# A two-block decode attention kernel: filler matmuls ahead of each exp, and the V products in one run

## The chip, the cores and the metric

The kernel runs on one core of one Trainium2 chip. The metric is device time in microseconds (us) of one execution; three runs of the kernel before gave 2033.15, 2031.56 and 2034.47 us, median 2033.15 us. The core's engines are named as in the profile: PE is TensorE (matmuls), PEld its weight loads, DVE VectorE, ACT ScalarE, POOL GpSimd, and SP the engine whose queue issues the transfers. "Clock" means the TensorE clock that the throttle granted, as a share of full speed.

## The reference

Two attention blocks, A and B, of the same shape; each is one decode step (one query position) over a cache:

```python
B, Sq, D = 2, 1, 640;  H, Sk, Dh = 32, 8192, 192        # bf16
q = (x @ wq).reshape(B, Sq, H, Dh).transpose(0, 2, 1, 3)
scores = jnp.einsum("bhqd,bhkd->bhqk", q, k_cache) * (Dh ** -0.5)
p = softmax(scores, axis=-1)
o = jnp.einsum("bhqk,bhkd->bhqd", p, v_cache)
out = o.transpose(0, 2, 1, 3).reshape(B, Sq, H * Dh) @ wo   # A and B concatenated
```

K and V are 2 x 32 x 8192 x 192 bf16 for each block, and every element is used once. The four caches are 805.3 MB of the 836.77 MB that the profile counts as read.

## The kernel before

The 2 blocks x 2 batches x 32 heads are handled two heads at a time: 64 **pairs**, i = 0 to 63. One pair's K is one transfer of 6144 KB into a buffer of 128 partitions (64 for each head, 128 positions in each), and so is its V. Three such buffers (`ring`, line 86) are filled in turn in the order K0, V0, K1, V1, ..., V61, K62, K63, V62, V63 (lines 155 to 169). All these transfers are issued by SP (line 134), strictly in that order, and each waits until the buffer's last contents have been used: by this rotation **K of pair i+2 waits for the last V product of pair i**, and **V of pair i+1 waits for the last multiplication of K of pair i**. Two loads of `wq` lead the stream, and eleven pieces of `wo` end it, in the buffers of K63, V62 and V63.

The order on each engine is written out by hand in the loop at line 382; each engine has a stream of its own, and waits are semaphores.

For pair i: K is taken in four quarters. `add_mul` (DVE, line 233) multiplies a quarter by the broadcast query into one of two `prod` buffers. `add_sum` (PE, line 238) adds the products over the head dimension, in 12 matmuls with the identity, each 128x512 moving columns, into one of two PSUM tiles `scps`. `add_red` (DVE, line 245) reduces the 16 columns that are left to scores. The DVE order is multiply 0, multiply 1, reduce 0, multiply 2, reduce 1, multiply 3, reduce 2, reduce 3; multiply 2 needs the buffer that sum 0 reads. `add_max` takes the maximum (DVE lines 250 and 251, POOL line 254), `add_exp` the exponentials (ACT, lines 259 to 266). `add_l` (PE, line 284) sums the denominators; it is the first PE instruction that waits for exp.

`add_pv` is the V product: 64 matmuls (line 278), each loading 34 columns of probabilities as weights and streaming 384 columns of V. Before the change it is cut in three: 52 matmuls follow `add_l` of the same pair, 6 follow sum 0 of the next pair and 6 follow sum 1 of the next pair. Only the last of the 64 signals `("pv", i)`, for which K of pair i+2 waits on SP. `add_od` and `add_on` (ACT line 294, DVE lines 298 to 302) normalise the output, and `add_place` (PE, line 312) puts it into the transposed layout for `wo`. `add_contract` (PE, line 327) multiplies by `wo` at the end.

Of the kernel before, what the change touches and what calls it, by code (L numbers as in the profile page):

```python
# [8 lines left out]
BF16 = mybir.dt.bfloat16  # L9
F32 = mybir.dt.float32  # L10
# [41 lines left out]
def build_kernel(nc, blocks, out):  # L52
# [8 lines left out]
    T = 128  # L61
# [19 lines left out]
    with ExitStack() as es:  # L81
        sb = lambda name, shape, dt: es.enter_context(nc.sbuf_tensor(name, shape, dt))
        ps = lambda name, shape, dt: es.enter_context(nc.psum_tensor(name, shape, dt))
# [17 lines left out]
        ident = sb("ident", [128, 128], BF16)  # L101
        selb = sb("selb", [34, 2, 128], BF16)
        place = sb("place", [2, 264], BF16)
        ones = sb("ones", [128, 1], F32)
        oallS = [sb(f"oallS{k}", [128, WR, 2], BF16) for k in range(NBLK)]
        out_sb = [sb(f"out_sb{k}", [34, NH2], BF16) for k in range(NBLK)]
        actd = sb("actd", [128, 2], F32)
# [3 lines left out]
        qps = ps("qps", [128, 512], F32)  # L111
        oall = ps("oall", [128, 512], F32)
        outps = ps("outps", [128, 512], F32)

        reg = {}
        S_sp = _Stream("sp", sem("s_sp"), reg)
        S_pe = _Stream("pe", sem("s_pe"), reg)
        S_act = _Stream("act", sem("s_act"), reg)
        S_dve = _Stream("dve", sem("s_dve"), reg)
        S_pool = _Stream("pool", sem("s_pool"), reg)  # L120
# [69 lines left out]
        def pr3(qd):  # L190
            return prod[qd % 2][:].rearrange("p (t d) -> p t d", d=Dh)

        def key(name, i, *rest):
            return (name, i) + rest if i >= 0 else None

        def before(i, qd, n):
            k = 4 * i + qd - n
            return (k // 4, k % 4) if k >= 0 else None
# [29 lines left out]
        def add_mul(i, qd):  # L228
            q = qt[i % 3][:].unsqueeze(1).broadcast_to([128, TQ, Dh])
            prev = before(i, qd, 2)  # L230
            w = [("k", i), ("qt", i)]
            w += [("s",) + prev] if prev else [("pr", 0, NQC - 1), ("pr", 1, NQC - 1)]
            S_dve.add(lambda eng: eng.tensor_tensor(pr3(qd), quarter(i, qd), q, ALU.mult), waits=w, sig=("m", i, qd))  # L233

        def add_sum(i, qd):
            def fn(eng):
                for j in range(NJ):
                    ins = eng.matmul(scps[qd % 2][:], ident[:], pr3(qd)[:, :, j * DG:(j + 1) * DG],  # L238
                                     start=(j == 0), stop=(j == NJ - 1))
                return ins  # L240
            prev = before(i, qd, 2)
            S_pe.add(fn, waits=[("m", i, qd), ("init",), ("r",) + prev if prev else None], sig=("s", i, qd))

        def add_red(i, qd):
            S_dve.add(lambda eng: eng.tensor_reduce(sc[i % 2][:, qd * TQ:(qd + 1) * TQ], scps[qd % 2][:], AXL.X, ALU.add),  # L245
                      waits=[("s", i, qd), key("exp", i - 2)], sig=("r", i, qd))

        def add_max(i):
            def fn(eng):
                eng.tensor_reduce(mp[i % 2][0:64, 0:1], sc[i % 2][0:64, :], AXL.X, ALU.max)  # L250
                return eng.tensor_reduce(mp[i % 2][64:128, 1:2], sc[i % 2][64:128, :], AXL.X, ALU.max)  # L251
            S_dve.add(fn, waits=[("r", i, 0), ("r", i, 1), ("r", i, 2), ("r", i, 3), key("ar", i - 2), ("init",)],
                      sig=("mx", i))
            S_pool.add(lambda eng: eng.partition_all_reduce(mg[i % 2][:], mp[i % 2][:], 128, bass.bass_isa.ReduceOp.max),  # L254
                       waits=[("mx", i), key("nb", i - 2)], sig=("ar", i))

        def add_exp(i):
            def fn_nb(eng):
                eng.activation(nb[i % 2][0:64, :], mg[i % 2][0:64, 0:1], ACTF.Identity, scale=-scale)  # L259
                return eng.activation(nb[i % 2][64:128, :], mg[i % 2][64:128, 1:2], ACTF.Identity, scale=-scale)  # L260
            S_act.add(fn_nb, waits=[("ar", i), key("exp", i - 2)], sig=("nb", i))

            def fn(eng):
                for h in range(2):
                    p0 = 64 * h
                    ins = eng.activation(pb[i % 2][p0:p0 + 64, :, h::32],  # L266
                                         sc[i % 2][p0:p0 + 64, :].rearrange("p (j a) -> p j a", a=2),
                                         ACTF.Exp, bias=nb[i % 2][p0:p0 + 64, :], scale=scale,
                                         accum_out=rs[i % 2][p0:p0 + 64, h:h + 1])
                return ins  # L270
            S_act.add(fn, waits=[("nb", i), ("r", i, 3), key("pv", i - 2), key("l", i - 2), ("init",)], sig=("exp", i))

        def pv_part(i, j0, j1):
            vv = ring[slot_of["v", i]][:].rearrange("p (j f) -> p j f", f=2 * Dh)

            def fn(eng):
                for j in range(j0, j1):
                    ins = eng.matmul(ops[i % 2][0:34, 0:2 * Dh], pb[i % 2][:, j, :], vv[:, j, :],  # L278
                                     start=(j == 0), stop=(j == T // 2 - 1))
                return ins  # L280
            return fn

        def add_l(i):
            S_pe.add(lambda eng: eng.matmul(ops[i % 2][0:2, 448:449], rs[i % 2][:], ones[:], start=True, stop=True),  # L284
                     waits=[("exp", i), key("on", i - 2), ("qe", 1, NQC - 1), ("init",)], sig=("l", i))

        def add_pv(i, j0, j1):
            w = [("exp", i), ("v", i)]
            if i == LAST and j0:
                w.append(("v2", i))  # L290
            S_pe.add(pv_part(i, j0, j1), waits=w, sig=("pv", i) if j1 == T // 2 else None)

        def add_od(i):
            S_act.add(lambda eng: eng.activation(oodd[i % 2][:], ops[i % 2][32:34, Dh:2 * Dh], ACTF.Identity),  # L294
                      waits=[("pv", i), key("on", i - 2)], sig=("od", i))

        def add_on(i):
            S_dve.add(lambda eng: eng.reciprocal(rc[i % 2][:], ops[i % 2][0:2, 448:449]),  # L298
                      waits=[("l", i), ("pv", i), key("on", i - 2)], sig=("rc", i))
            S_dve.add(lambda eng: eng.tensor_tensor(oodd[i % 2][:], ops[i % 2][0:2, 0:Dh], oodd[i % 2][:], ALU.add),  # L300
                      waits=[("od", i)], sig=("ad", i))
            S_dve.add(lambda eng: eng.tensor_scalar(on[i % 2][:], oodd[i % 2][:], rc[i % 2][:], None, ALU.mult),  # L302
                      waits=[("rc", i), ("ad", i), key("pl", i - 2)], sig=("on", i))
# [42 lines left out]
        for blk in range(NBLK):  # L346
# [5 lines left out]
        S_pool.add(lambda eng: eng.affine_select(out=place[:], in_=place[:], compare_op=ALU.is_equal, fill=0.0, base=-128,  # L352
                                                 pattern=[[1, 264]], channel_multiplier=-4), waits=[("pl0",)])
        S_pool.add(lambda eng: eng.memset(ones[:], 1.0))
        for t in rs + pb:
            S_pool.add((lambda t: lambda eng: eng.memset(t[:], 0.0))(t))
        for t in mp:
# [7 lines left out]
        def fn_x(eng):  # L365
            for c in range(DC):
# [4 lines left out]
                  waits=[("xp",)], sig=("xT",))  # L371
# [5 lines left out]
                    add_q(i)  # L377
                    add_qt(i)

        J = T // 2  # L380
        J1, J2 = J - 12, J - 6
        for i in range(NP):
            mid = 0 < i < LAST
            add_mul(i, 0)
            add_mul(i, 1)
            add_sum(i, 0)
            if mid:
                add_pv(i - 1, J1, J2)
            add_red(i, 0)
            add_mul(i, 2)  # L390
            add_sum(i, 1)
            if mid:
                add_pv(i - 1, J2, J)
                add_od(i - 1)
            add_red(i, 1)
            add_mul(i, 3)
            add_sum(i, 2)
            add_red(i, 2)
            if mid:
                add_on(i - 1)  # L400
            if i + 2 < NP:
                add_q(i + 2)
                add_qt(i + 2)
            add_sum(i, 3)
            if mid:
                add_place(i - 1)
            add_red(i, 3)
            add_max(i)
            add_exp(i)
            if i < NP - 2:  # L410
                add_l(i)
                add_pv(i, 0, J1)
        for i in (NP - 2, NP - 1):
            add_l(i)
            if i == LAST:
                add_pv(i, 0, J // 2)
                add_pv(i, J // 2, J)
            else:
                add_pv(i, 0, J)
            add_od(i)  # L420
            add_on(i)
            if i == NP - 2:
                add_place(i)
# [77 lines left out]
```

## Time and profile before

| what | value |
|---|---|
| median of three runs | 2033.15 us (2031.56 to 2034.47) |
| the profiled execution, its own time | 2037.92 us |
| its span, first to last instruction | 2036.1 us |
| read from memory | 836.77 MB, 411 GB/s over the span |
| PE, DVE, ACT busy | 1616.5 us (79%), 1081.5 us (53%), 187.1 us (9%) |
| packets' time of the loading queue, share of 16 engines | 97.1% |
| mean granted TensorE clock | 0.916 |

Busy times of PE come from records whose ends are modelled, so 79% is no measure of how near PE is to its limit. The share of the DMA engines is the time that packets took; a packet that takes longer than others makes this share larger and not the transfer faster, so GB/s is to be read beside it.

### The profile page before, as it was taken

Reading aid. Unit: us, or ns where it says so; the run is one execution under the profiler, and the core shown is the slowest. Engines: PE = TensorE matmul, PEld = TensorE weight load, DVE = VectorE, ACT = ScalarE, POOL = GpSimd, SP = SyncE. Lnnn points to the kernel's source line nnn. Section 1 sums busy time; section 2 is a strip of 40 time slices with the busy share of each in tenths; the row PEclk is TensorE's granted clock in tenths of the full one; section 3 lists DMA queues with packets and bytes.
Section 4 is the critical chain, followed back from the end, with each engine's and each line's share of the span. In section 5 each row is a group of like instructions: output and inputs, shape, how many; then the busy total and the mean of one; then the engine's idle time right before and its main releaser. Section 6 shows DMA issues by size and latency. Waiting matters only on the chain.

```text
span 2036.1 us, 17767 instructions
## 1 busy us (share of the span) xinstructions
PE 1616.5 (79%) x7933; PEld 748.8 (37%) x7933; DVE 1081.5 (53%) x833; ACT 187.1 (9%) x610; POOL 32.2 (2%) x82
## 2 busy tenths in 40 slices
PE   5878887878878887887878878887877777877877
PEld 1333333333333433333333333333333333333334
DVE  0645655645655655655655645645645645645660
ACT  2101001001011001001001001001001001001000
POOL 1000000000000000000000000000000000000000
PEclk9998988888998988989888988988999999898989
DMA  9999999999999999999999999999999999999998
GB/s 414 430 409 416 404 430 394 402 427 406 402 431 406 424 410 416 404 427 421 403 418 417 408 428 398 416 405 405 404 426 419 403 421 402 390 426 393 426 401 381
DMA packets 20836, 837.91 MB, mean 412 GB/s; under 512 B 2316, under 2 KB 2584, under 8 KB 2968
## 3 DMA queue, kind: packets, MB, share of 16 engines
q1 hardware_dynamic: 20744, 836.78, 97.1%
q8 instruction: 62, 1.02, 0.2%
q14 instruction: 14, 0.11, 0.0%
q10 hardware_dynamic: 16, 0.01, 0.0%
HBM read 836.77 MB, written 0.01 MB: 411 GB/s over the span
## 4 chain that ended last, share of the span: by engine, by line
issue 62%; DMA 20%; PE 12%; DVE 5%; POOL 1%; SPq 0%; ACT 0%; POOLq 0%; DVEq 0%
DMA ring<-in_B_k_cache_dram 17%; PE scps L238 7%; DVE prod L233 4%; PE ops L278 4%; DMA prod<-in_B_wq_dram 2%; DMA ring<-in_B_wo_dram 1%; PE ops L205 1%; POOL mg L254 1%; DVE sc L245 0%; SPq L134 0%; ACT pb L266 0%; POOLq L43 0%; DVE mp L251 0%; PE ops L284 0%; ACT out_sb L335 0%
## 5 line engine op out<-in xcount | busy, mean ns | idle before, releaser
L233 DVE TENSOR_TENSOR prod<-ring,qt 128x6144 bf16<-128x6144 bf16 x256 | 852.7, 3351 | 757.9 <-DMA ring<-in_B_k_cache_dram 354.3
L238 PE MATMUL scps<-prod,ident 128*128 128x512 bf16 x3072 | 762.5, 402 | 172.6 <-DVE prod L233 170.4
L278 PE MATMUL ops<-ring,pb 128*34 128x384 bf16 x4096 | 788.1, 354 | 0.0
L278 PEld LDWEIGHTS ops<-ring,pb 128*34 128x34 bf16 x4096 | 416.0, 105 | 359.9 <-issue 151.4
L238 PEld LDWEIGHTS scps<-prod,ident 128*128 128x128 bf16 x3072 | 292.1, 102 | 592.5 <-DVE prod L233 213.1
L245 DVE TENSOR_REDUCE sc<-scps 128x32 f32<-128x512 f32 x256 | 175.7, 686 | 147.0 <-PE scps L238 146.8
L284 PE MATMUL ops<-ones,rs 128*2 128x1 f32 x128 | 12.2, 164 | 211.8 <-ACT pb L266 211.8
L294 ACT ACTIVATE oodd<-ops 2x192 f32<-2x192 f32 x64 | 20.6, 321 | 1323.0 <-PE ops L278 1323.0
L284 PEld LDWEIGHTS ops<-ones,rs 128*2 128x2 f32 x128 | 5.5, 82 | 219.3 <-ACT pb L266 218.8
L266 ACT ACTIVATE pb<-sc,nb 64x128 bf16<-64x128 f32 x128 | 81.4, 636 | 3.1
L254 POOL PARTITION_ALL_REDUCE mg<-mp x64 | 25.8, 404 | 1948.2 <-DVE mp L251 1948.2
L266 ACT ACTIVATION_READ_ACCUMULATOR pb<-sc,nb 64x1 f32 x128 | 38.3, 299 | 0.0
L205 PE MATMUL ops<-ring,xT 128*2 128x512 bf16 x96 | 29.0, 431 | 11.7 <-DMA prod<-in_A_wq_dram 10.2
L259 ACT ACTIVATE nb<-mg 64x1 f32<-64x1 f32 x64 | 13.0, 203 | 275.6 <-POOL mg L254 275.6
L224 ACT ACTIVATE qt<-qps 64x192 bf16<-64x192 f32 x64 | 20.7, 323 | 176.3 <-PE qps L218 176.3
L218 PE MATMUL qps<-qrow,selb 2*128 2x384 bf16 x64 | 21.2, 332 | 1.4 <-ACT qt L225 0.8
L300 DVE TENSOR_TENSOR oodd<-ops,oodd 2x192 f32<-2x192 f32 x64 | 20.9, 326 | 0.4 <-ACT oodd L294 0.4
L302 DVE TENSOR_SCALAR on<-oodd,rc 2x192 bf16<-2x192 f32 x64 | 19.7, 307 | 2.3
L225 ACT ACTIVATE qt<-qps 64x192 bf16<-64x192 f32 x64 | 20.8, 325 | 0.8
L312 PEld LDWEIGHTS oall<-on,place 2*128 2x128 bf16 x256 | 10.3, 92 | 28.1 <-issue 26.6
L298 DVE RECIPROCAL rc<-ops 2x1 f32<-2x1 f32 x64 | 9.4, 146 | 20.3 <-PE ops L278 20.3
L327 PE MATMUL outps<-ring,oallS 128*2 128x320 bf16 x192 | 14.5, 299 | 7.0 <-DMA ring<-in_B_wo_dram 6.9
(33 smaller groups left out, 125.8 us busy)
## 6 DMA issues: line engine op xcount, KB each, us to landing
ring<-in_A_k_cache_dram SPq DMA_DIRECT2D x32, 6144.0 KB, 18.5
ring<-in_A_v_cache_dram SPq DMA_DIRECT2D x32, 6144.0 KB, 30.2
ring<-in_B_k_cache_dram SPq DMA_DIRECT2D x32, 6144.0 KB, 18.9
ring<-in_B_v_cache_dram SPq DMA_DIRECT2D x31, 6144.0 KB, 30.3
ring<-in_A_wq_dram SPq DMA_DIRECT2D x1, 6144.0 KB, 17.6
ring<-in_B_wq_dram SPq DMA_DIRECT2D x1, 6144.0 KB, 35.4
ring<-in_B_v_cache_dram SPq DMA_DIRECT2D x2, 3072.0 KB, 25.2
ring<-in_A_wo_dram SPq DMA_DIRECT2D x2, 3040.0 KB, 20.5
```

The source lines that it names most:

```text
L205: ins = eng.matmul(ops[n % 2][32 * blk:32 * blk + 2, 0:QC], xT[:, c, 2 * blk:2 * blk + 2], src, start=(c == 0), stop=(c == DC - 1))
L218: S_pe.add(lambda eng: eng.matmul(qps[:, 0:2 * Dh], selb[r0:r0 + 2, b, :], qrow[r0:r0 + 2, 2 * ii * Dh:(2 * ii + 2) * Dh], start=True, sto ...
L224: eng.activation(qt[i % 3][0:64, :], qps[0:64, 0:Dh], ACTF.Identity)
L225: return eng.activation(qt[i % 3][64:128, :], qps[64:128, Dh:2 * Dh], ACTF.Identity)
L233: S_dve.add(lambda eng: eng.tensor_tensor(pr3(qd), quarter(i, qd), q, ALU.mult), waits=w, sig=("m", i, qd))
L238: ins = eng.matmul(scps[qd % 2][:], ident[:], pr3(qd)[:, :, j * DG:(j + 1) * DG], start=(j == 0), stop=(j == NJ - 1))
L245: S_dve.add(lambda eng: eng.tensor_reduce(sc[i % 2][:, qd * TQ:(qd + 1) * TQ], scps[qd % 2][:], AXL.X, ALU.add), waits=[("s", i, qd), key( ...
L254: S_pool.add(lambda eng: eng.partition_all_reduce(mg[i % 2][:], mp[i % 2][:], 128, bass.bass_isa.ReduceOp.max), waits=[("mx", i), key("nb" ...
L266: ins = eng.activation(pb[i % 2][p0:p0 + 64, :, h::32], sc[i % 2][p0:p0 + 64, :].rearrange("p (j a) -> p j a", a=2), ACTF.Exp, bias=nb[i % ...
L278: ins = eng.matmul(ops[i % 2][0:34, 0:2 * Dh], pb[i % 2][:, j, :], vv[:, j, :], start=(j == 0), stop=(j == T // 2 - 1))
L294: S_act.add(lambda eng: eng.activation(oodd[i % 2][:], ops[i % 2][32:34, Dh:2 * Dh], ACTF.Identity), waits=[("pv", i), key("on", i - 2)], ...
L300: S_dve.add(lambda eng: eng.tensor_tensor(oodd[i % 2][:], ops[i % 2][0:2, 0:Dh], oodd[i % 2][:], ALU.add), waits=[("od", i)], sig=("ad", i))
```

## The change

A constant tile `filler` of ones and a PSUM tile `fillps` are added. `add_fill(12)` puts 12 matmuls (identity by `filler`, 128x512 columns) on PE in every pair, behind the last sum and the placing matmuls and ahead of `add_l`; they wait only for the initial setting of the constants, and their result is never read. The V product is no longer cut: all 64 matmuls of pair i follow `add_l` of pair i, and `add_od` follows at once on ACT. `add_place` is written two lines later, which leaves it behind sum 3 on PE. The order of transfers on SP and of all operations on DVE stays.

```diff
+        filler = sb("filler", [128, 512], BF16)
...
+        fillps = ps("fillps", [128, 512], F32)
...
+        def add_fill(n):
+            def fn(eng):
+                for _ in range(n):
+                    ins = eng.matmul(fillps[:], ident[:], filler[:], start=True, stop=True)
+                return ins
+            S_pe.add(fn, waits=[("init",)])
...
+        S_pool.add(lambda eng: eng.memset(filler[:], 1.0))
...
-        J = T // 2
-        J1, J2 = J - 12, J - 6
         for i in range(NP):
             mid = 0 < i < LAST
             add_mul(i, 0)
             add_mul(i, 1)
             add_sum(i, 0)
-            if mid:
-                add_pv(i - 1, J1, J2)
             add_red(i, 0)
             add_mul(i, 2)
             add_sum(i, 1)
-            if mid:
-                add_pv(i - 1, J2, J)
-                add_od(i - 1)
             add_red(i, 1)
...
             add_sum(i, 3)
+            add_red(i, 3)
+            add_max(i)
             if mid:
                 add_place(i - 1)
-            add_red(i, 3)
-            add_max(i)
             add_exp(i)
+            add_fill(12)
             if i < NP - 2:
                 add_l(i)
-                add_pv(i, 0, J1)
+                add_pv(i, 0, T // 2)
+                add_od(i)
```

More of the change, by code (lines that the diff above doesn't have):

```diff
@@ L415, in build_kernel @@
             if i == LAST:
-                add_pv(i, 0, J // 2)
-                add_pv(i, J // 2, J)
+                add_pv(i, 0, T // 4)
+                add_pv(i, T // 4, T // 2)
             else:
-                add_pv(i, 0, J)
+                add_pv(i, 0, T // 2)
             add_od(i)
```

## The prediction

> **What bounds the kernel now.** I read the page's chain and its DMA lines first. The chain runs through the DMA of K, sums and V products (where it says "issue", the view has lost its thread), and the queue moves 411 GB/s over the span. Is that its limit? At the start the queue is always fed, so I asked for the busy times of three stretches, one there:
>
> ```profile
> core 0: us, PE busy (x) PEld busy (x) DVE busy (x) ACT busy (x) POOL busy (x), PEclk, DMA share, GB/s
> ...
> 23.00:85.00 62.00, 49.57 (x206) 19.30 (x205) 16.71 (x11) 17.70 (x36) 0.37 (x1) 0.92 1.00 431
> ...
> 1020.00:1960.00 940.00, 747.06 (x3646) 347.87 (x3647) 515.14 (x394) 81.22 (x277) 10.63 (x30) 0.92 0.97 412
> 2001.00:2030.00 29.00, 23.02 (x240) 13.43 (x242) 1.10 (x4) 0.98 (x3) 0.00 (x0) 1.00 1.00 421
> ```
>
> The last column is the thing to see: 431 GB/s with a fed queue, 412 in the steady state. Landings say it more sharply. K0, V0 and K1 land at 2.9 + 52.6 = 55.5, 37.45 + 32.6 = 70.05 and 57.1 + 27.5 = 84.6 us (issue plus "DMA to landing" of each): **14.55 us for each 6144 KB load that waits in the queue**. Two loads are 29.1 us. But the first multiplication of pair 1 starts at 84.59 and that of pair 62 at 1949.25 us: 30.57 us for each of 61 pairs. So 1.47 us of each pair is not transfer. The timeline of two neighbouring pairs shows where:
>
> ```profile
> 949.74 0.65 PE L278 MATMUL ops<-ring,pb 128*34 128x384 bf16 x3
> ...
> 950.42 0.33 SPq L134 DMA_DIRECT2D ring<-in_A_k_cache_dram  x1
> ...
> 953.74 0.33 SPq L134 DMA_DIRECT2D ring<-in_A_v_cache_dram  x1
> ...
> 956.47 0.27 PE L312 MATMUL oall<-on,place 2*128 2x48 bf16 x4
> ...
> 960.15 0.19 PE L284 MATMUL ops<-ones,rs 128*2 128x1 f32 x2 [3.41 <-ACT pb L266]
> ...
> 968.47 6.63 DVE L233 TENSOR_TENSOR prod<-ring,qt 128x6144 bf16<-128x6144 bf16 x2 [10.59 <-DMA ring<-in_A_k_cache_dram]
> ...
> 980.04 1.15 PE L278 MATMUL ops<-ring,pb 128*34 128x384 bf16 x6
> ...
> 981.22 0.33 SPq L134 DMA_DIRECT2D ring<-in_A_k_cache_dram  x1
> ...
> 1000.69 6.63 DVE L233 TENSOR_TENSOR prod<-ring,qt 128x6144 bf16<-128x6144 bf16 x2 [12.34 <-DMA ring<-in_A_k_cache_dram]
> ```
>
> SP issues a K the moment the last V product has ended (949.74 + 0.65, then 950.42; 980.04 + 1.15, then 981.22). The V load ahead of it, issued at 923.32 and 953.74, lands 30.5 and 29.5 us later, at 953.8 and 983.2. The K issued 3.4 us before that landing arrives 14.6 us after it, which is the bare transfer; the K issued 2.0 us before arrives 17.4 us after, 2.9 us late. In a 2 us window there (980 to 982 us) the queue moves 74 GB/s. So the kernel is a loop on the edge of its transfers: a K must be issued about 3.4 us ahead of the V landing, and the last 12 V products, behind sums 0 and 1 of the next pair, come about 12 us after the K landing (968.47 to 981.19 is 12.7), just too late.
>
> **The change, part by part.**
>
> *V products in one run.* The 64 products in one run take 10.57 us in the trace (pair 62, at 1989.64, clock 1.00); 52 take 8.62. The row for pair 0 shows the new order of the sums, since nothing stands between them there: from its first sum (60.61) to line 284 (79.41) is 18.80 us, of which 1.65 is a cold start (24 matmuls take 7.04 us, two groups of 2.70 each when warm). So from first sum to the last V product is 17.15 + 0.12 + 10.57 = **27.84 us** at full clock. The first sum comes 3.4 us after the K landing (968.47 to 971.88), so the V run ends 31.2 us after its own K has landed, 2.1 us after the next K if those come every 29.1 us. K of pair i+2 is issued then, 14.55 - 2.1 = 12.4 us ahead of the V landing where 3.4 are enough: 9 us in hand, a wait that no longer counts. V has itself landed 14.55 us after K, and exp ends about 20.5 us after it, so the run waits for no V. What is late next: PE must end the run before the next first sum, 27.84 against 29.1 us, **1.3 us in hand per pair**. That is the thin place of the change.
>
> *SP's queue.* Order and number of transfers stay. V of pair i+1 stands behind K of pair i+1 and waits for multiplication 3 of pair i, which ends about 14 us after that K (15.7 in the pair at 968.47, with a cold first sum); its turn in the queue comes at 29.1. Nothing there is late.
>
> *Fillers.* Twelve matmuls of 128x512 take 2.70 us at full clock, like a sum, and lie in PE's wait for exp (3.41 us in the row at 960.15, 211.8 us in 62 such waits). At half clock they take 5.1 us (weight loads 0.427 us apart at 972 us), 1.4 to 1.7 us over that cover. What they may bring: after these waits the clock is sometimes 0.50 (990 to 996 us), and 52 products then take 11.15 instead of 8.62 us. With fillers PE stands idle there for about 1 us. I cost them at 0, with 1.7 us a pair as the other end.
>
> *The rest, at nothing.* `add_place` keeps its place behind sum 3. `add_od` waits on ACT ahead of the next pair's qt, and ends 3 us into that pair, where qt is made after sum 2. One more constant on POOL (0.2 us, or 3.75 like the pair of pb settings at the other end) is hidden: POOL is done at 17.3, PE first needs it at 38.1. In the last pairs 2.7 us of fillers and the whole V run precede the pieces of `wo`, but K63, V62 and V63 are still queued then (29 us) and 3 to 14 us of `wo` behind them.
>
> *Sum,* from the profiled execution. Up to K1 (84.6) nothing changes. K62: 84.6 + 61 x 29.1 = 1859.7. K63, V62, V63: 3 x 14.55 = 43.7. `wo`: 2 x 7.86 MB at 421 GB/s = 37.4. From the last landing to the end, 2.6 as now (2033.5 to 2036.1). Span **1943.4 us**, against 2036.1; with the 1.8 us outside the span (2037.92 - 2036.1) **1945 us**. The median of the runs shown is 4.8 us below the profiled one; I don't carry that over, as the sum is now one of transfers and not of a loop that varies.
>
> The Trainium skill, DMA: Bandwidth & Descriptors (Where 436 GB/s comes from), gives 435.2 GB/s as the ceiling of the 16 ports. By it a load takes an estimated 14.46 us and the sum is 11 us less, 1934; the trace agrees within 1% (432 for K0 to K1).
>
> **The rivals.**
>
> *A, forecast:* the queue is fed throughout. 1936 to 1960. Chance 0.69.
>
> *B, the clock eats the 1.3 us.* With the cold first sum of pair 0 in every pair the PE loop is 27.84 + 1.65 = 29.5 us: 0.4 x 62 = 25 us, 1970. For it: mean clock 0.916 now. Against: the waits of 3.4 us and more go, and PE works some 24 of 29 us. 1960 to 2020, chance 0.11.
>
> *C, slower: PE becomes the bound.* If in addition every V run starts cold (+2.53, the row of 11.15), the loop is 32.0 us and the time 1945 + 62 x 2.9 = 2125. The point that decides is 30.57 us, 2.7 us a pair over the full-clock loop. Place: the first sums, which now stand behind all 64 products. For it: V products no longer bridge the pauses of 0.8 to 1.5 us between sums. Against: in pair 0 sums 2 and 3, behind pauses of 1.46 and 0.84 us, take 2.77 and 2.76 us, full speed. Chance 0.09. The Trainium skill, TensorE: Matmul & The Clock Gate (A second HAM failure mode), says that short idles between groups of matmuls can make the clock oscillate; by that rule C would come, and the rows of pair 0 do not show it.
>
> *D, K loads are slow in themselves* and not because the queue ran dry. If half of the 1.47 us stays, 1945 + 62 x 0.74 = 1991. Against: K1, queued early, took 14.55. Chance 0.07.
>
> *E, the change does nothing:* the gap turns up elsewhere in the queue (V's wait). 2030 to 2037, chance 0.04.
>
> **How the numbers follow.** Forecast A, 1945. The range goes from 1936 (435 GB/s) to 1985, which takes in most of B; D's upper part, C and E are outside, some 0.2. Two runs of this kernel differ by up to 0.15%, so 0.2% is about what can be told from no change. Faster: A, B and D, 0.87. Same: E, 0.04. Slower: C, 0.09.
>
> **What the profile would show.** Right: about 430 GB/s in every slice; DVE line 233 still waiting for K, but with K's time from issue to landing near 27 us instead of 18.5; first multiplications 29.1 us apart; line 278 in groups of 64 of about 10.6 us; clock near 1.0. For B or C: PE line 238 follows line 278 without a wait, DVE no longer waits for K, and K's time to landing falls back to 18 us. For D: K waits in the queue for long and pairs still take over 29.5 us. I am wrong at the root if the queue is always full and the pace is still 30.5 us.

## The result and the profile after

The changed kernel takes **1955.1 us** (median of 4 runs, 1954.86 to 1955.62); the kernel before, in runs on the same chip, 2033.81 us (2031.56 to 2036.67). The ratio is **0.9613, 95% interval 0.9596 to 0.9629**: 3.9% faster. Forecast: 1945 us, range 1936 to 1985. The profiled execution took 1955.21 us, its span is 1953.5 us.

From the page of the changed kernel: the clock and the memory rate in 40 slices, and the median time of K and V loads from issue to landing (last column).

```profile
span 1953.5 us, 19240 instructions
...
PEclk9999999999999999999999999999999999999999
...
GB/s 415 432 434 430 432 432 428 433 430 433 433 432 433 432 431 432 433 431 432 430 432 431 432 432 433 433 430 431 432 432 432 425 430 433 432 431 428 432 428 348
...
ring<-in_A_k_cache_dram SPq DMA_DIRECT2D x32, 6144.0 KB, 26.6
ring<-in_A_v_cache_dram SPq DMA_DIRECT2D x32, 6144.0 KB, 29.2
```

Every slice but the first and the last is between 425 and 434 GB/s, where the steady state was 412. A K now waits 26.6 us from issue to landing, 8 us more than before: that wait is the good sign, as it is time in the queue behind a load that is still moving. One pair in the timeline shows the reason:

```profile
932.69 6.63 DVE L235 TENSOR_TENSOR prod<-ring,qt 128x6144 bf16<-128x6144 bf16 x2 [10.56 <-DMA ring<-in_A_k_cache_dram]
935.14 0.33 SPq L136 DMA_DIRECT2D ring<-in_A_k_cache_dram  x1
...
936.11 2.76 PE L240 MATMUL scps<-prod,ident 128*128 128x512 bf16 x12 [1.00 <-DVE prod L235]
...
950.23 2.54 PE L288 MATMUL fillps<-filler,ident 128*128 128x512 bf16 x11 [0.16 <-issue]
...
953.49 0.19 PE L293 MATMUL ops<-ones,rs 128*2 128x1 f32 x2 [0.72 <-ACT pb L268]
...
953.61 10.58 PE L280 MATMUL ops<-ring,pb 128*34 128x384 bf16 x64
961.74 6.63 DVE L235 TENSOR_TENSOR prod<-ring,qt 128x6144 bf16<-128x6144 bf16 x2 [10.53 <-DMA ring<-in_A_k_cache_dram]
964.21 0.33 SPq L136 DMA_DIRECT2D ring<-in_B_k_cache_dram  x1
```

K is issued 2.5 us after the K landing (932.69 to 935.14), not 11 to 12.7. Pairs come 29.05 us apart here. PE rests 0.72 us ahead of the denominators and 1.00 us ahead of the first sum, so the thin place is as thin as forecast: first sum to last V product is 28.1 us (936.11 to 964.19). (One of the 12 fillers is missing from the records.)

### The profile page after: what moved, and what is told of

Its sections match the earlier page's. It is cut to its first block, busy times and chain, and to the rows that moved or that the text cites. A ratio compares the mean times of both kernels' runs of the same rounds, so it can differ in the third digit from the quotient of the medians.

```text
span 1953.5 us, 19240 instructions
## 1 busy us (share of the span) xinstructions
PE 1632.2 (84%) x8637; PEld 785.1 (40%) x8701; DVE 1078.5 (55%) x833; ACT 187.3 (10%) x610; POOL 32.6 (2%) x83
## 4 chain that ended last, share of the span: by engine, by line
issue 89%; DMA 4%; PE 3%; DVE 2%; POOL 1%; SPq 0%; ACT 0%; POOLq 0%; DVEq 0%
DMA prod<-in_B_wq_dram 2%; DVE prod L235 2%; PE ops L280 2%; DMA ring<-in_B_k_cache_dram 1%; POOL mg L256 1%; DMA ring<-in_B_wo_dram 1%; PE ops L207 1%; PE scps L240 1%; DVE sc L247 0%; SPq L136 0%; PE fillps L288 0%; ACT pb L268 0%; POOLq L43 0%; DVE mp L253 0%; ACT out_sb L344 0%
## 5 line engine op out<-in xcount | busy, mean ns | idle before, releaser
L240 PE MATMUL scps<-prod,ident 128*128 128x512 bf16 x3072 | 710.1, 381 | 232.1 <-DVE prod L235 232.1
L280 PE MATMUL ops<-ring,pb 128*34 128x384 bf16 x4096 | 676.8, 326 | 0.0
L240 PEld LDWEIGHTS scps<-prod,ident 128*128 128x128 bf16 x3072 | 280.0, 98 | 640.0 <-DVE prod L235 334.4
L280 PEld LDWEIGHTS ops<-ring,pb 128*34 128x34 bf16 x4096 | 394.6, 98 | 259.5
L288 PE MATMUL fillps<-filler,ident 128*128 128x512 bf16 x704 | 162.4, 379 | 9.9 <-issue 9.8
L288 PEld LDWEIGHTS fillps<-filler,ident 128*128 128x128 bf16 x768 | 70.0, 98 | 78.4
L226 ACT ACTIVATE qt<-qps 64x192 bf16<-64x192 f32 x64 | 20.7, 323 | 685.5 <-PE qps L220 685.5
L293 PE MATMUL ops<-ones,rs 128*2 128x1 f32 x128 | 12.1, 164 | 44.8 <-ACT pb L268 44.8
L321 PEld LDWEIGHTS oall<-on,place 2*128 2x128 bf16 x256 | 10.3, 92 | 28.1 <-issue 26.6
## 6 DMA issues: line engine op xcount, KB each, us to landing
ring<-in_A_k_cache_dram SPq DMA_DIRECT2D x32, 6144.0 KB, 26.6
ring<-in_A_v_cache_dram SPq DMA_DIRECT2D x32, 6144.0 KB, 29.2
ring<-in_B_k_cache_dram SPq DMA_DIRECT2D x32, 6144.0 KB, 26.6
ring<-in_B_v_cache_dram SPq DMA_DIRECT2D x31, 6144.0 KB, 29.2
```

What stands on the lines that cost most here:

```text
L226: eng.activation(qt[i % 3][0:64, :], qps[0:64, 0:Dh], ACTF.Identity)
L288: ins = eng.matmul(fillps[:], ident[:], filler[:], start=True, stop=True)
```

## The experiments

Two explanations fit the result. **ISSUE:** the last V product ends sooner, so K is issued in time; fillers and clock are incidental. **CLOCK:** the fillers hold the clock (0.916 to 0.997). The ratios below are to runs of the kernel before made beside each kernel (medians 2031.55 to 2037.92 us).

**1. No fillers, one run of V products.**

```diff
             add_exp(i)
-            add_fill(12)
```

> The changed kernel without the 12 fillers; all 64 V products still follow exp in one run. Theory ISSUE (the gain comes from K being issued earlier, because the last V product ends some 10 us sooner): the queue stays fed, 1955 us, or up to 1975 where cold V runs push the PE loop (28.1 us in the changed kernel) over the 29.25 us of the transfers; K's time to landing stays near 26 us. Theory CLOCK (the gain comes from the clock that the fillers hold, 0.916 to 0.997): every V run starts cold again, +2.5 us, the loop is 30.2 to 30.6 us, 2010 to 2034 us.

Measured: 1989.56 us, ratio 0.9802 (0.976 to 0.9843), mean clock 0.919. Neither theory had it: more than half of the gain without any filler, but 34 us lost to the changed kernel. The timeline:

```profile
1014.00 5.35 PE L240 MATMUL scps<-prod,ident 128*128 128x512 bf16 x24
1014.10 0.33 SPq L136 DMA_DIRECT2D ring<-in_B_k_cache_dram  x1
...
1031.18 13.50 PE L280 MATMUL ops<-ring,pb 128*34 128x384 bf16 x64
...
1032.83 6.63 DVE L235 TENSOR_TENSOR prod<-ring,qt 128x6144 bf16<-128x6144 bf16 x2 [4.04 <-DMA ring<-in_B_k_cache_dram]
...
1044.61 5.35 PE L240 MATMUL scps<-prod,ident 128*128 128x512 bf16 x24
```

The V run takes 13.50 us where it took 10.58; in the loop no V run is shorter than 11.86 us. Sums 0 and 1 follow it in one group of 24 with no wait in brackets: their products have long been ready, and PE is late. This turn of PE (its work for one pair) is 30.6 us (1014.00 to 1044.61); the mean of four turns, 1000.55 to 1120.02 us, is 29.87, above the 29.25 of the transfers. The clock in three stretches (last three values: clock, DMA share, GB/s):

```profile
1027.50:1031.00 3.50, 0.15 (x4) 0.04 (x2) 1.24 (x3) 1.90 (x7) 0.35 (x1) 0.90 1.04 449
1031.00:1036.00 5.00, 4.94 (x18) 2.42 (x19) 3.17 (x1) 0.01 (x2) 0.00 (x0) 0.50 1.00 433
1036.00:1044.00 8.00, 8.00 (x47) 4.69 (x46) 3.46 (x2) 0.00 (x0) 0.00 (x0) 0.93 0.98 424
```

While PE waits for exp (0.15 us busy of 3.5) the clock begins to fall (0.90); the first 5 us of the run have half of it (0.50). So the fillers do matter in this order of work, through the PE loop.

**2. The V products' place alone.** The kernel before, cut 58 + 6 instead of 52 + 6 + 6, no fillers:

```diff
-        J1, J2 = J - 12, J - 6
+        J1 = J - 6
...
             add_sum(i, 0)
             if mid:
-                add_pv(i - 1, J1, J2)
+                add_pv(i - 1, J1, J)
+                add_od(i - 1)
...
             add_sum(i, 1)
-            if mid:
-                add_pv(i - 1, J2, J)
-                add_od(i - 1)
```

> The kernel before with one thing changed: 58 V products follow exp and the last 6 follow sum 0 of the next pair (none follow sum 1); no fillers. ISSUE: K is issued 7.3 us (9 with a cold first sum) after the K landing, 5.5 to 7 us ahead of the V landing where about 3.4 are enough, so the queue stays fed: 1955 to 1965 us although the clock stays near 0.92. CLOCK: nothing holds the clock, so 2025 to 2035 us.

Measured: **1954.56 us**, ratio 0.9629 (0.9594 to 0.9663). Twelve matmuls, each moved ahead of one sum, give the whole gain, with a clock (0.92) as low as before. Lines of its page, then one of its busy times (last three values: clock, DMA share, GB/s):

```profile
PEclk9889989999989989989989989989988989988999
...
ring<-in_A_k_cache_dram SPq DMA_DIRECT2D x32, 6144.0 KB, 21.7
```

```profile
1020.00:1900.00 880.00, 729.03 (x3562) 344.04 (x3560) 517.95 (x396) 79.04 (x269) 13.78 (x30) 0.92 1.00 431
```

Clock 0.92, 431 GB/s: CLOCK alone is dead as the cause. The V run starts cold here too, but it is off the path:

```profile
1011.75 12.32 PE L278 MATMUL ops<-ring,pb 128*34 128x384 bf16 x58
...
1020.03 6.63 DVE L233 TENSOR_TENSOR prod<-ring,qt 128x6144 bf16<-128x6144 bf16 x2 [10.67 <-DMA ring<-in_B_k_cache_dram]
...
1024.01 2.76 PE L238 MATMUL scps<-prod,ident 128*128 128x512 bf16 x12
```

The 58 products take 12.32 us and hold up the first sum by only 0.6 us (its product is ready at 1020.03 + 3.35 = 1023.38), and DVE still waits 10.67 us for K, against 4.04 us in experiment 1.

**3. The issue of K made late again**, everything else as changed, fillers too:

```diff
-            free[s] = [("m", i, 3)] if kind == "k" else [("pv", i)]
+            free[s] = [("m", i, 3)] if kind == "k" else [("pv", i)] + ([("s", i + 1, 2)] if i < LAST else [])
```

> The changed kernel with fillers and one V run, but SP issues K of pair i+2 only after sum 2 of pair i+1, 13.2 us after the K landing (before the change: 11 to 12.7). PE and its clock are left as they are. ISSUE: the queue runs dry again, a pair takes 13.2 + 17.5 to 18.3 = 30.7 to 31.5 us, 2043 to 2092 us. CLOCK: 1955 us.

Measured: 2166.57 us, ratio 1.0672 (1.0634 to 1.0711). The direction is ISSUE's; the size is more than the 2043 to 2092 given. Some stretches have pairs of 30.5 us, near the 30.7 worked out, others of 32 to 34 us, where most first sums are cold:

```profile
1321.19 0.33 SPq L136 DMA_DIRECT2D ring<-in_B_k_cache_dram  x1
...
1339.38 6.63 DVE L235 TENSOR_TENSOR prod<-ring,qt 128x6144 bf16<-128x6144 bf16 x2 [13.03 <-DMA ring<-in_B_k_cache_dram]
...
1342.80 6.67 PE L240 MATMUL scps<-prod,ident 128*128 128x512 bf16 x24 [3.47 <-DVE prod L235]
```

K lands 18.2 us after issue; PE has rested 3.47 us when the first product is ready, and its 24 matmuls take 6.67 instead of 5.35 us (8.17 in the pair ahead, behind a rest of 3.51). That makes the next K later still, and the rest longer. I had left this feedback out.

**4. The same, after sum 1** instead of sum 2 (`("s", i + 1, 1)`):

> As late2, but SP issues K of pair i+2 after sum 1 of pair i+1, 9.4 us after the K landing instead of 2.5 (changed kernel) or 13.3 (late2, which took 2166.57 us). Theory ISSUE with a threshold: 14.6 - 9.4 = 5.2 us ahead of the V landing is more than the 3.4 us that were enough before the change, so the queue stays fed and the time is that of the changed kernel, 1955 us within 5. Rival (any delay of K costs, in proportion): about half of the way to late2, 2050 us.

Measured: 1955.94 us, ratio 0.9638 (0.9611 to 0.9664). K is issued 9.5 us after the K landing (992.20 to 1001.68 in its timeline), seven later than in the changed kernel, and it costs at most 0.8 us. So lateness costs nothing up to an edge, which lies between 9.5 us (this) and 11 to 12.7 (before); beyond it the cost is steep.

**5. Fillers alone**, in the order before (52 + 6 + 6):

```diff
             add_exp(i)
+            add_fill(12)
             if i < NP - 2:
                 add_l(i)
                 add_pv(i, 0, J1)
```

The filler's tiles and its constant are added as in the change.

> The kernel before (V products cut 52 + 6 + 6) with the 12 fillers alone ahead of the denominators' matmul. ISSUE: the last V products stay behind sums 0 and 1, K is issued 11 to 12.7 us after the K landing as before, 2015 to 2050 us; V runs start warm and end sooner, so PE may rest longer ahead of the first sum, which can then be cold more often. CLOCK: 1955 to 1975 us.

Measured: 2074.84 us, ratio 1.0218 (1.0181 to 1.0256), **slower than before**, beyond the range, though the mean clock rises to 0.940. Its timeline:

```profile
1007.67 8.62 PE L280 MATMUL ops<-ring,pb 128*34 128x384 bf16 x52
1017.64 6.63 DVE L235 TENSOR_TENSOR prod<-ring,qt 128x6144 bf16<-128x6144 bf16 x2 [12.37 <-DMA ring<-in_A_k_cache_dram]
...
1021.06 5.30 PE L240 MATMUL scps<-prod,ident 128*128 128x512 bf16 x12 [4.77 <-DVE prod L235]
...
1031.28 0.33 SPq L136 DMA_DIRECT2D ring<-in_B_k_cache_dram  x1
```

The V run is fast now (8.62 us) and ends early, so PE rests 4.77 us ahead of the first sum, and that sum takes 5.30 us instead of 2.76. K is issued 13.6 us after the landing. The fillers moved the cold stretch from the V run to the first sum, which is on the path. In the kernel before, a cold V run of 11.15 us (at 990.74) still left PE 2.21 us of rest ahead of its first sum, so there it cost nothing.

**6. How many fillers.** `add_fill(6)`, `add_fill(24)` and `add_fill(36)` in the changed kernel.

> The changed kernel with 6 fillers instead of 12. They cover 1.3 us of PE's 3.4 us wait for exp, 2.1 us are left. Theory THRESHOLD (the clock falls only after an idle time of about 3 us; first sums behind 2.4 us of idle ran at full speed in late2): V runs start warm, 1955 us within 5. Rival SHARE (the clock follows the busy share, so half the fillers do half the work): about 1970 us, between 1955 with 12 and 1989.56 with none.

> The changed kernel with 24 fillers instead of 12. They end 1.84 us after exp does (12 end 0.72 us before it, 12 more are 2.56 us). Theory PE LOOP: the loop on PE grows from 27.8 to 29.65 us, just over the 29.25 us of the transfers: 0.4 x 61 = 24 us, 1979 us (1960 to 1995), PE no longer waits for the first product of a pair. Rival (fillers are harmless beside a bound of transfers, or help the clock further): 1955 us.

> The changed kernel with 36 fillers. PE LOOP: 27.8 + 1.84 + 2.56 = 32.2 us a pair, 2.95 x 61 = 180 us over the changed kernel, 2135 us (2115 to 2150), slower than before the change. Rival: 1955 to 1980 us.

Measured: 6 fillers 1955.26 us, ratio 0.9635 (0.9603 to 0.9667); 24: 1968.27 us, 0.9698 (0.967 to 0.9725), 13 us where 24 were worked out; 36 (two runs): 2135.33 us, 1.0522 (1.0476 to 1.0567). With 6, PE still rests 2.02 us ahead of every V run. One run is then slow, the next shown at full speed:

```profile
982.90 0.19 PE L293 MATMUL ops<-ones,rs 128*2 128x1 f32 x2 [2.02 <-ACT pb L268]
983.02 12.26 PE L280 MATMUL ops<-ring,pb 128*34 128x384 bf16 x64
...
1012.27 0.19 PE L293 MATMUL ops<-ones,rs 128*2 128x1 f32 x2 [2.02 <-ACT pb L268]
...
1012.39 10.57 PE L280 MATMUL ops<-ring,pb 128*34 128x384 bf16 x64
```

Of 62 V runs, 35 take 10.57 us and 27 take 12.1 to 12.3, with a half-clock stretch inside (0.50 from 984.5 to 986 us). So THRESHOLD has the time right and not its reason, "V runs start warm": a rest of 2.02 us does not keep the clock in every pair. As SHARE has it, half the fillers do part of the work; the time does not show it, because PE's turn, 28.1 + 1.7 x 27/62 = 28.8 us by estimate, stays under the 29.25 of the transfers. With 36, PE's turn is 32.1 us (1013.37 to 1045.44, the starts of two V runs), DVE waits 2.52 us for its K and the products wait for PE:

```profile
1005.60 7.72 PE L288 MATMUL fillps<-filler,ident 128*128 128x512 bf16 x35 [0.16 <-issue]
...
1009.10 6.63 DVE L235 TENSOR_TENSOR prod<-ring,qt 128x6144 bf16<-128x6144 bf16 x2 [2.52 <-DMA ring<-in_A_k_cache_dram]
...
1013.25 0.19 PE L293 MATMUL ops<-ones,rs 128*2 128x1 f32 x2
...
1013.37 10.57 PE L280 MATMUL ops<-ring,pb 128*34 128x384 bf16 x64
...
1023.87 5.35 PE L240 MATMUL scps<-prod,ident 128*128 128x512 bf16 x24
```

This is the end that rival C named, PE as the bound, reached by fillers and not by the clock: the 1.3 us in hand are real, and what is above them goes straight into the time: (32.1 - 29.25) x 61 = 174 us, measured 180.

**7. Cut 58 + 6 with fillers:** experiment 2 with `add_fill(12)` ahead of `add_l`, and the filler's tiles and constant.

> The cut 58 + 6 (which took 1954.56 us at a clock of 0.92) with the 12 fillers ahead of the denominators' matmul. If the fillers only repair the clock of the long V run, they have nothing to repair here, as K is already issued in time: 1955 us within 3, at a higher clock. Rival (the clock is worth something of its own): 1945 to 1950 us. If fillers make PE rest longer ahead of the first sum, as in the order before (52 + 6 + 6), first sums go cold but the 5 us in hand absorb it.

Measured: 1954.91 us, ratio 0.9598 (0.9549 to 0.9647), clock 0.977. A clock 0.06 higher than in experiment 2 and the same time: the clock has no worth of its own here. Nothing tried beats the changed kernel by more than its runs differ; three other kernels, cut 58 + 6 without and with fillers and the one with 6 fillers (1954.56, 1954.91, 1955.26 us), meet the same floor, 430 to 431 GB/s.

**8. Why 14.62 us a load and not 14.55.** The changed kernel with 160 tiny constant settings per pair on the idle POOL, in a tile `spare` that nothing reads:

```diff
+            for c in range(160):
+                S_pool.add((lambda c: lambda eng: eng.memset(spare[:, c:c + 1], 0.0))(c), ...)
```

> The changed kernel with 160 small constant settings more on POOL per pair, in a tile that nothing reads; POOL is idle there. They only add 10240 instructions that must be fetched. The question is why a queued load took 14.62 us over the whole run and not the 14.55 of its start. Theory FETCH: instruction fetch shares the 16 transfer engines (68 packets of 16 KB, 0.2% of their time in the changed kernel); some 40 packets more are about 2.6 us of the mean engine, 1956.5 to 1960 us, and the page's instruction line shows above 100 packets. Rival (fetch is free beside the loads): 1955 us within 0.7.

Measured: 2002.16 us, ratio 0.9831 (0.9788 to 0.9873). Both theories fail: the cost is 47 us, not 0 and not 2.6. Page lines:

```profile
q1 hardware_dynamic: 20744, 836.78, 98.5%
q8 instruction: 68, 1.11, 0.2%
q14 instruction: 94, 0.77, 0.1%
...
ring<-in_A_k_cache_dram SPq DMA_DIRECT2D x32, 6144.0 KB, 28.5
```

K waits 28.5 us in the queue, so the queue is fed; 80 instruction packets more (94, against 14) take a tenth of a percent of 16 engines. Yet the rate from 1020 to 1900 us is 421 GB/s. The page's slices show that it was not so from the start:

```profile
GB/s 417 429 433 427 435 428 433 433 422 429 415 403 424 416 423 419 421 419 419 425 421 427 413 424 423 415 427 429 415 410 420 418 423 420 417 428 418 424 408 314
```

Up to about 400 us the rate is as high as without the bursts. But the landings are late from the start: from 115.47 to 445.04 us, 11 pairs, first multiplications are 29.96 us apart on average (29.25 in the changed kernel). So one part of each load falls behind while the rest runs ahead in the queue, until it has nothing more to load. The trace's semaphore records agree: a load is complete after 16 marks, and from 450 us on the last comes 8.6 us (median) after the fifteenth, against 0.07 us in the changed kernel.

Two more kernels ask whether it is what POOL writes: 20 settings of 8 columns (the same bytes), and 160 of a single element.

> The changed kernel with 20 settings of 8 columns on POOL per pair instead of pool160's 160 of one column: the same bytes written, an eighth of the instructions (1280 in all). pool160 took 2002.16 us, 47 us over the changed kernel, although its loads were queued in time (K's time to landing 28.5 us). Theory COUNT (the number of instructions costs, by fetch or otherwise): an eighth of 47, about 1961 us. Theory BYTES (what POOL writes gets in the way of what the loads write): 2002 us as in pool160.

> As pool160 with the same 10240 instructions, each setting one element in one partition instead of one in each of 128. COUNT: 2002 us as in pool160. BYTES: about 1955 us, as a 128th is written.

Measured: 1955.3 us, ratio 0.9611 (0.9569 to 0.9654), and 2003.05 us, 0.9848 (0.9796 to 0.99). BYTES is dead. COUNT has the direction, but 1280 instructions cost 0.2 us, not 6, so it is not in proportion; whether the length of a burst (160 take 4.67 us) or the number in all decides, no run separates. Why one part of each load falls behind stays open. Instruction fetch is not excluded: FETCH was costed as a mean over 16 engines, and if the 80 packets all delayed the same part, 47 us would be 0.59 us for each.

## Why the prediction was right, point by point

*What bounds.* Right: the queue ran dry because K was issued too late. Experiments 2, 3 and 4 show it from both sides, with no filler added or taken away.

*The V run's cost and the thin place.* Right: forecast 27.84 us from first sum to last product, measured 28.1; K issued 2.1 us after the landing by forecast, 2.5 measured; 1.3 us in hand by forecast, 1.0 us of rest measured; experiment 6 shows where it ends.

*Fillers at 0:* right, and here the prediction said too little: it gave no price for leaving them out. They are worth 34 us in this order, as they repair a loop that the long run itself has made tight; the full clock that its 10.57 us presuppose was there only with them. In time 6 do as well as 12, and in the order before they cost 41 us.

*Rival B and C,* a clock that eats the margin: did not come in the changed kernel, but experiment 1 is C's cold V run, without its cold first sums. When does the clock fall? First sums start at half speed after rests of 3.47 us (experiment 3) and 4.77 us (experiment 5). After 3.41 us, 17 of 62 V runs are at full speed throughout before the change (8.62 us) and none in experiment 1. After 2.02 us, with 6 fillers, 35 of 62 are. The Trainium skill, TensorE: Matmul & The Clock Gate (The HAM clock gate), says that a rest of about one window of 3.4 us brings the half clock; the traces agree in most pairs with such a rest (45 of 62 before the change, all in experiment 1), and show the half clock after 2.02 us too, in 27 of 62 pairs. The Trainium skill's rule on the same page (A second HAM failure mode), by which short rests between groups unsettle the clock, is not borne out in the changed kernel: rests of 0.5 to 1.1 us between sums, mean clock 0.997.

*Rivals D and E:* excluded. Queued K loads are as fast as V loads (K lands at 932.69, V at 918.00 + 29.2 = 947.2, the next K at 961.74 us), and V is issued 14.4 us after the K landing (932.69 to 947.08), long before its turn.

*The sum.* The span came out 10.1 us longer than forecast (1953.5 against 1943.4). By its own terms: start to the first multiplication of pair 1, 84.68 us (forecast 84.6). Pair 1 to pair 62, 84.68 to 1868.82 us, is 61 x 29.25 us (forecast 29.1): **+9.1 us, the mis-sized term**. I took 14.55 us a load from two landings at the start, where the mean over the run is 14.62. The rest, 84.7 us (forecast 83.7), is +1.0. The timeline of DVE shows how the 0.07 us come about:

```profile
991.62 6.63 DVE L235 TENSOR_TENSOR prod<-ring,qt 128x6144 bf16<-128x6144 bf16 x2 [11.37 <-DMA ring<-in_B_k_cache_dram]
...
1021.42 6.63 DVE L235 TENSOR_TENSOR prod<-ring,qt 128x6144 bf16<-128x6144 bf16 x2 [11.27 <-DMA ring<-in_B_k_cache_dram]
```

From 961.74 us to the first line and from there to the second are 29.88 and 29.80 us. Of the 61 steps, 45 are 28.95 to 29.08 us, as forecast, and 16 are 29.5 to 30.05, mostly two in a row every seven or eight pairs. So the load's own time was right, and the term left out is a delay that comes back. Its cause was not settled; instruction fetch may be a part (the page gives it 0.2% of 16 engines, some 0.03 us a load by the same share). The median I did not carry over was rightly left: the runs of this kernel differ by 0.8 us, those of before by up to 27 us over all runs (2021.56 to 2048.55).

The end shows where a little more lies. Two stretches of 2 us of the kernel after, then two of the kernel before (last two values: DMA share and GB/s):

```profile
1944.00:1946.00 2.00, 1.25 (x16) 0.61 (x16) 0.00 (x0) 0.00 (x0) 0.00 (x0) 1.00 0.53 220
...
1948.00:1950.00 2.00, 0.84 (x10) 0.35 (x10) 0.00 (x0) 0.00 (x0) 0.00 (x0) 1.00 0.22 80
```

```profile
2028.00:2030.00 2.00, 0.92 (x14) 0.40 (x12) 0.00 (x0) 0.00 (x0) 0.00 (x0) 1.00 0.98 393
2030.00:2032.00 2.00, 1.02 (x18) 0.46 (x14) 0.00 (x0) 0.00 (x0) 0.00 (x0) 1.00 0.49 176
```

Before, the transfers run out within about 4 us (a share of 0.98 at 2028 to 2030, 0.06 at 2032 to 2034 us); now they take some 9 (0.93 at 1941 to 1943, 0.11 at 1949 to 1951 us). The 16 marks of a load drift apart in the changed kernel, from 1.9 us at 84.7 to 9.1 us at 1868.8 us, and widen with the delays above (3.9, 4.7 and 5.4 us at 493.7, 523.5 and 553.3 us); before, they stay within 0.5 to 4.0 us. A reading that no run tested: parts of a transfer that never stand still together drift apart, and the last one sets the end.

## What to carry to other kernels

In a loop of loads and work, measure by how much the issue of the next load leads the landing of the one ahead of it: up to an edge lateness is free, past it the whole delay and its consequences (cold matmuls, still later issue) go into the time. Ask first which single instruction releases the buffer, and move that one; here twelve matmuls, each moved ahead of one sum, were worth 79 us, and everything else in the change was a repair of what the larger move had made tight. Fillers for the clock paid only where the cold stretch lay on the path (34 us); in the cut 58 + 6 they gained nothing, and in the order before they moved the rest, and the cold, to a place where it cost 41 us.

## What the runs showed that was not expected

- Fillers alone made the kernel 2.2% slower while raising its mean clock from 0.916 to 0.940: a mean clock says nothing of which matmuls were slow.
- 10240 tiny instructions on an otherwise idle POOL, in bursts of 160, cost a transfer-bound kernel 47 us with the queue always fed, whether they write 128 partitions or one; one of the 16 completion marks of each load then came 8.6 us behind the rest. 1280 in bursts of 20 cost 0.2 us.
- A rest of 2.02 us in every pair left 35 of 62 V runs at full speed and gave 27 a half-clock stretch, and the time did not change.
- Loads queued without a pause ran at 430 to 432 GB/s, stretch by stretch, for 1.8 ms. The Trainium skill, DMA: Bandwidth & Descriptors (Where 436 GB/s comes from), gives 435 as the ceiling; the traces come within 1%.
